# Scores of a causal chunk as three quarter blocks a head pair, and a chunk's values moved to the next iteration

## The chip, the core and the metric

The kernel runs on one core of a Trainium2 chip. The metric is the device time of one execution in microseconds (us); lower is better. Five engines run their own instruction streams in order: TensorE (PE, matmuls; PEld is its weight load), VectorE (DVE), ScalarE (ACT), GpSimdE (POOL) and SyncE (SP, which here only issues DMAs). They wait for each other by semaphores.

## The reference, cut to what matters

A linear attention with a complex, per-channel decay feeds a top-1 mixture of experts. Batch 4, 8 heads, 768 steps, 48 channels a head:

```python
for t in range(S):
    ar, ai = a_re_n[:, :, t, :, None], a_im_n[:, :, t, :, None]
    S_re, S_im = ar * S_re - ai * S_im + k_t (x) v_t, ar * S_im + ai * S_re
    y[:, :, t] = einsum('bhd,bhde->bhe', q[:, :, t], S_re)
...
e_idx = argmax(x @ w_gate, axis=1)          # x: y as 3072 rows of 384
for e in range(E):                          # 8 experts, 384 -> 1024 -> 384
    h = maximum(x[mask] @ w1[e], 0.0)
    out[mask] = gate_w * eom[mask, e] * (h @ w2[e])
```

## The kernel before, in words

The kernel has two stages. The attention stage (0 to about 272 us) walks over 24 chunks of 128 steps, six for each batch entry; the expert stage (about 283 us to the end) walks over eight experts. The change touches the first alone.

For chunk i, `main()` (L796) asks for these steps:

- `turn(i, "k")` and `turn(i, "q")` (L607): DVE multiplies the decayed k or q by cosine and sine (L611, tiles `kc`, `qc`), PE turns the eight heads (L95, into the PSUM banks `tr`, of which there are two), and ACT copies each bank of four heads out (L621, tiles `kt`, `qt`).
- `score(i, 0)` and `score(i, 1)` (L646), four heads each: PE makes a 128x128 matrix of keys by queries for each head (L653, PSUM tile `sc`), and DVE multiplies four of them by the causal mask (L654, 512 columns). Of each matrix the quarter with late keys and early queries is masked away.
- `state(i)` (L625): PE adds keys times values into the running state (L633, L638, tile `st`), in matmuls that give 32 partitions, and DVE scales it (L642).
- `values(i)` (L660): PE makes scores times values (L667) and queries times state (L673), heads in pairs. The even head's output lies on partitions 0 to 47 of the tile `xo`, the odd head's on 64 to 111. ACT copies it out (L677, `xt`).
- `finish(i)` (L682, L688) turns `xt` back (again into a `tr` bank) and stores it to `xd`; `gates(i)` (L233) and `chosen(i)` (a PE transpose of `ls`, L95, and L240) make the routing logits.

Beside this, groups of three chunks are prepared: logarithms, exponentials and arctangents on ACT and DVE, two running sums on PE (L510 and L563, tile `cs`), and a one-row `carry` from chunk to chunk, which is sent by a DMA that SP issues (L573) before DVE adds it into the next chunk (L545).

The order is not the order of the code. Within the attention loop a scheduler places the instructions of each engine, by a priority that follows from where `main()` and the side steps ask for them and by when it reckons that operands and buffers are ready. The stream it makes is fixed when the program is built; the engines then run it in order. After chunk 19 the lists of the first experts are made: table writes (L1059), the reading back of the lists, and the gather of expert 0's rows (L1104), which PE turns in L1012; the rows of the last two chunks come in through L763 (DVE) and L998 (PE). Then the experts begin (L1225).

## Time and profile before

| what | us |
|---|---|
| median of three runs (lowest, highest) | 530.51 (528.88, 531.61) |
| the profiled execution, its own time | 532.94 |
| its span in the trace | 531.1 |
| attention stage: last `xo` matmul begins | 272.0 |
| first expert matmul (L1225) | 283.12 |
| PE busy over the span | 493.5 |
| DVE busy, ACT busy | 337.3, 319.0 |

A "busy" time of PE contains the tail of each matmul, so that a busy PE isn't PE at its best pace; the time from one matmul's start to the next tells the pace. In the trace each fp32 matmul of the program, transposes aside, is two passes. A chain row gives a start, a length and what stood there, with the number of passes behind an x.

### The profile page before, as it was taken

To read this page: it belongs to the slowest core of one execution; us is meant where nothing else is said; L and a number is where in the kernel's file an instruction comes from. 1 tells how busy PE (TensorE), PEld (TensorE's weight loads), DVE (VectorE), ACT (ScalarE), POOL (GpSimd) and SP (SyncE) were. 2 spreads that over 40 slices of the span, in tenths; PEclk is the share of its full clock that TensorE was granted. 3 is DMA by queue.
4 is the path that set the end of the run, shared out by engine and by line. 5 is a ranking of instruction groups with operands and counts; after the bars stand their busy time and mean duration, and the time that the engine had idled before them with its cause. 6 is when DMAs were issued, how large, how long until landed. Compare 5 with 4: busy or idle time off the path is not lost.

```text
span 531.1 us, 11170 instructions
## 1 busy us (share of the span) xinstructions
PE 493.5 (93%) x4297; PEld 420.3 (79%) x4297; DVE 337.3 (64%) x775; ACT 319.0 (60%) x603; POOL 121.1 (23%) x131
## 2 busy tenths in 40 slices
PE   2799897998999999999899999999999999999992
PEld 0376565776777778878678889999999999999992
DVE  4578869895998899987685646355453726345220
ACT  7689678985879888767533447355453727354220
POOL 4000201030040503051350554412333222011112
PEclk9799989998999999999999999999999999999997
DMA  8664452534334321014560576525263644330001
GB/s 274 199 231 150 74 165 69 161 77 114 124 76 136 58 90 41 29 31 136 138 207 0 149 191 198 153 101 206 47 209 114 200 123 147 139 135 30 21 22 45
DMA packets 47523, 63.86 MB, mean 120 GB/s; under 512 B 12383, under 2 KB 39290, under 8 KB 47460
## 3 DMA queue, kind: packets, MB, share of 16 engines
q1 hardware_dynamic: 39332, 53.64, 33.8%
q0 software_dynamic: 8128, 9.42, 6.1%
q8 instruction: 36, 0.59, 0.5%
q14 instruction: 27, 0.22, 0.2%
HBM read 53.92 MB, written 9.88 MB: 120 GB/s over the span
## 4 chain that ended last, share of the span: by engine, by line
PE 57%; issue 17%; DMA 7%; DVE 7%; POOL 4%; ACT 4%; SPq 1%; POOLq 0%; DVEq 0%; ACTq 0%
PE up L1225 13%; PE acc L1163 12%; PE tr L95 8%; PE sc L653 4%; PE cs L563 4%; PE xo L667 3%; POOL out_dram L1176 3%; PE cs L510 3%; DMA carry<-ai 2%; PE xo L673 2%; PE st L638 2%; DMA ar<-in_a_re_dram 2%; PE cs L565 1%; POOL rows L1104 1%; PE xt L95 1%
## 5 line engine op out<-in xcount | busy, mean ns | idle before, releaser
L1230 DVE SCALAR_TENSOR_TENSOR hl<-up,hh 128x464 fp32r<-128x464 f32 (+7 forms) x64 | 37.7, 589 | 68.8 <-ACT hh L1229 67.5
L1229 ACT ACTIVATE hh<-up 128x464 fp32r<-128x464 f32 (+7 forms) x64 | 33.1, 518 | 74.0 <-PE up L1225 72.7
L1225 PE MATMUL up<-xh,w1h 128*128 128x464 f32 (+7 forms) x192 | 68.6, 357 | 0.0
L1225 PE MATMUL up<-xl,w1h 128*128 128x464 f32 (+7 forms) x192 | 67.6, 352 | 0.0
L1225 PE MATMUL up<-xh,w1l 128*128 128x464 f32 (+7 forms) x192 | 67.5, 351 | 0.0
L1163 PE MATMUL acc<-hh,w2h 128*128 128x464 f32 (+6 forms) x168 | 61.4, 366 | 0.0
L1176 POOL DMA_INDIRECT out_dram<-y,sid x28 | 31.8, 1135 | 124.5 <-ACT y L1198 121.6
L1163 PE MATMUL acc<-hl,w2h 128*128 128x464 f32 (+6 forms) x168 | 59.4, 356 | 0.0
L1163 PE MATMUL acc<-hh,w2l 128*128 128x464 f32 (+6 forms) x168 | 59.3, 353 | 0.0
L653 PE MATMUL sc<-qt,kt 96*128 96x128 f32 x384 | 51.2, 277 | 0.0
L653 PEld LDWEIGHTS sc<-qt,kt 96*128 96x128 f32 x384 | 47.3, 192 | 2.4 <-issue 1.1
L1104 POOL DMA_INDIRECT rows<-xd,sid x28 | 37.3, 1333 | 51.4 <-DVE w1l L203 22.6
L1059 POOL DMA_INDIRECT table<-entry,addr x20 | 31.4, 1571 | 65.3 <-DVE addr L1055 59.0
L203 DVE TENSOR_TENSOR w1l<-raw,w1h 128x512 fp32r<-128x512 f32 x48 | 30.5, 686 | 20.4 <-ACT w1h L202 17.3
L667 PE MATMUL xo<-scores,v 128*48 128x128 f32 x384 | 41.4, 279 | 0.0
L202 ACT CAST w1h<-raw 128x512 fp32r<-128x512 f32 x48 | 26.9, 619 | 17.0 <-DMA raw<-in_moe_w_dram 17.0
L1225 PEld LDWEIGHTS up<-xl,w1h 128*128 128x128 f32 x192 | 36.0, 188 | 1.2 <-DVE xl L1137 0.3
L1225 PEld LDWEIGHTS up<-xh,w1l 128*128 128x128 f32 x192 | 36.1, 188 | 1.0
L1225 PEld LDWEIGHTS up<-xh,w1h 128*128 128x128 f32 x192 | 36.1, 188 | 0.9
L203 DVE TENSOR_TENSOR w2l<-raw,w2h 128x512 fp32r<-128x512 f32 x48 | 30.5, 686 | 9.8 <-ACT w2h L202 7.4
L533 POOL COPY rcs<-rcs 24x48 f32<-24x48 f32 (+2 forms) x10 | 5.8, 579 | 134.0 <-DMA rcs<-re 86.9
L654 DVE TENSOR_TENSOR scores<-sc,mask 128x512 f32<-128x512 f32 x48 | 32.6, 681 | 5.0 <-PE sc L653 4.5
(214 smaller groups left out, 1125.2 us busy)
## 6 DMA issues: line engine op xcount, KB each, us to landing
raw<-in_moe_w_dram SPq DMA_DIRECT2D x32, 768.0 KB
ar<-in_a_re_dram SPq DMA_DIRECT2D x24, 192.0 KB
ai<-in_a_im_dram SPq DMA_DIRECT2D x24, 192.0 KB
k<-in_k_dram SPq DMA_DIRECT2D x24, 192.0 KB
q<-in_q_dram SPq DMA_DIRECT2D x24, 192.0 KB
v<-in_v_dram SPq DMA_DIRECT2D x24, 192.0 KB
xd<-xn SPq DMA_DIRECT2D x24, 192.0 KB
rows<-xd,sid POOLq DMA_INDIRECT x28
```

What stands on the lines that cost most here:

```text
L95: return nc.tensor.transpose(out=out, in_=in_, identity=ident[p0:p0 + n, p0:p0 + n])
L203: ins = nc.vector.tensor_tensor(out=lo[:, s], in0=raw[:, s], in1=hi[:, s].bitcast(F32), op=ALU.subtract)
L653: nc.tensor.matmul(sp[:, j * P:(j + 1) * P], r["kt"][:D2, h, :], r["qt"][:D2, h, :], start=True, stop=True)
L654: nc.vector.tensor_tensor(out=r["s"][:, 4 * hh:4 * hh + 4, :], in0=sp.rearrange("p (h t) -> p h t", t=P), in1=mask.unsqueeze(1).broadcast_ ...
L667: nc.tensor.matmul(op[u * DP:u * DP + D, j * P:(j + 1) * P], vt[c][:, h * D:(h + 1) * D], r["s"][:, h, :], start=True, stop=(cc == 0))
L1059: ins = nc.gpsimd.indirect_dma_start(out=table, out_offset=bass.IndirectOffsetOnAxis(ap=addr[:, c:c + 1], axis=0), in_=entry[:, c, :], in_ ...
L1104: nc.gpsimd.indirect_dma_start(out=rows[e % 2][:n, i, :], out_offset=None, in_=xd[:known], in_offset=bass.IndirectOffsetOnAxis(ap=ids[:n, ...
L1163: nc.tensor.matmul(accs[kt][:, :cap], w[:, cs], a, start=(ft == 0 and s == 0), stop=(ft == FT - 1 and s == 2))
L1176: ins = nc.gpsimd.indirect_dma_start(out=out, out_offset=bass.IndirectOffsetOnAxis(ap=ids(e)[:n, i:i + 1], axis=0), in_=y[:n, :], in_offse ...
L1225: nc.tensor.matmul(up[:, :cap], w[:, kt, :], x[:, kt, :], start=(m == 0), stop=(m == 3 * KT - 1))
L1229: nc.scalar.activation(out=hh, in_=up[:, :cap], func=AF.Relu)
L1230: nc.vector.scalar_tensor_tensor(out=hl, in0=up[:, :cap], scalar=0.0, in1=hh.bitcast(F32), op0=ALU.max, op1=ALU.subtract)
```

## The change

Three things are changed.

1. Scores. Keys and queries are cut in halves of 64. For each pair of heads (e even, o odd) four matmuls make 192 columns instead of 256: on partitions 0 to 63 the early keys of e with all queries and the late keys of o with the late queries, on partitions 64 to 127 the early keys of o with all queries and the late keys of e with the late queries. Each gives 64 partitions. The DVE mask works on 384 columns for four heads instead of 512, with a mask built of three blocks.
2. Values. For each pair the early queries take one matmul a head over all 128 partitions, with weights that are zero in the other head's half (`vz`), and the late queries one matmul a head, the even one with `v`, the odd one with a tile whose halves are swapped (`vs`). So a pair has four matmuls of 64 columns instead of two of 128. `vz` and `vs` are filled by four further DMAs a chunk; v arrives in memory with the even heads first. POOL builds the new mask and zeroes eight half tiles at the start.
3. Order of asking. `main()` asks in each iteration for values(i-1), score(i), state(i), gates(i-1), turn(i+1), finish(i-1) and chosen(i-1).

```diff
+            first_v = [pre.tile([P, H, D], F32, name=f"vz{n}") for n in range(VBUFS)]
+            for t in first_v:
+                nc.gpsimd.memset(t[HALF:, 0:HP, :], 0.0)
+                nc.gpsimd.memset(t[:HALF, HP:H, :], 0.0)
+            other_v = [pre.tile([P, HP, D], F32, name=f"vs{n}") for n in range(VBUFS)]
...
+            def loads_halves(i):
+                rows = v.rearrange("b (c x t) h d -> (b c) x t h d", x=2, t=HALF)[i]
+                z, o = first_v[i % VBUFS], other_v[i % VBUFS]
+                nc.sync.dma_start(out=z[:HALF, 0:HP, :], in_=rows[0, :, 0:HP, :])
+                nc.sync.dma_start(out=z[HALF:, HP:H, :], in_=rows[0, :, HP:H, :])
+                nc.sync.dma_start(out=o[:HALF], in_=rows[1, :, HP:H, :])
+                nc.sync.dma_start(out=o[HALF:], in_=rows[0, :, HP:H, :])
...
-                for j in range(4):
-                    h = 4 * hh + j
-                    nc.tensor.matmul(sp[:, j * P:(j + 1) * P], r["kt"][:D2, h, :], r["qt"][:D2, h, :], start=True, stop=True)
+                for j in range(2):
+                    e, o = 4 * hh + 2 * j, 4 * hh + 2 * j + 1
+                    kt, qt = r["kt"][:D2], r["qt"][:D2]
+                    to = sp[:, j * 3 * HALF:(j + 1) * 3 * HALF].rearrange("p (x t) -> p x t", t=HALF)
+                    parts = qt.rearrange("p h (x t) -> p h x t", t=HALF)
+                    nc.tensor.matmul(to[:HALF, 0:2, :], kt[:, e, :HALF], parts[:, e], start=True, stop=True)
+                    nc.tensor.matmul(to[HALF:, 0:3:2, :], kt[:, o, :HALF], parts[:, o], start=True, stop=True)
+                    nc.tensor.matmul(to[:HALF, 2, :], kt[:, o, HALF:], qt[:, o, HALF:], start=True, stop=True)
+                    nc.tensor.matmul(to[HALF:, 1, :], kt[:, e, HALF:], qt[:, e, HALF:], start=True, stop=True)
                 nc.vector.tensor_tensor(
-                    out=r["s"][:, 4 * hh:4 * hh + 4, :], in0=sp.rearrange("p (h t) -> p h t", t=P),
-                    in1=mask.unsqueeze(1).broadcast_to([P, 4, P]), op=ALU.mult)
+                    out=r["s"][:, 2 * hh:2 * hh + 2, :], in0=sp[:, :6 * HALF].rearrange("p (j t) -> p j t", j=2),
+                    in1=masks.rearrange("p x t -> p (x t)").unsqueeze(1).broadcast_to([P, 2, 3 * HALF]), op=ALU.mult)
...
                     for u in range(2):
-                        h = 2 * j + u
                         nc.tensor.matmul(
-                            op[u * DP:u * DP + D, j * P:(j + 1) * P], vt[c][:, h * D:(h + 1) * D], r["s"][:, h, :],
-                            start=True, stop=(cc == 0))
+                            op[u * DP:u * DP + D, j * P:j * P + HALF], vz[:, at_v(2 * j + u), :], by_block[:, 0, :],
+                            start=True, stop=(cc == 0), skip_group_check=True)
+                    for u in range(2):
+                        nc.tensor.matmul(
+                            op[u * DP:u * DP + D, j * P + HALF:(j + 1) * P], vs[:, j, :] if u else vt[c][:, j * D:(j + 1) * D],
+                            by_block[:, 1 + u, :], start=False, stop=(cc == 0), skip_group_check=True)
...
+                    if live(i - 1):
+                        yield from values(i - 1)
                     if live(i):
                         yield from score(i, 0)
                         yield from score(i, 1)
...
+                        yield from state(i)
+                    if live(i - 1):
+                        yield from gates(i - 1)
+                    if live(i + 1):
+                        need(i + 1)
+                        yield from turn(i + 1, "k")
+                        yield from turn(i + 1, "q")
+                    if live(i - 1):
+                        yield from finish(i - 1)
+                        yield from chosen(i - 1)
```

How the streams move is seen on PE, first, in the middle of the attention stage. Before, these eight rows follow each other there (`tr` are transposes, `sc` scores, `st` the state, `xo` the values; the numbers behind the names count buffers):

```order
L95 MATMUL tr_1883<-ident_71,kc1_162 96x128 x4
L653 MATMUL sc_1890<-qt0_165,kt0_166 128x128 x4
L95 MATMUL tr_1897<-ident_71,qc1_161 96x128 x4
L95 MATMUL tr_1907<-ident_71,qc1_161 96x128 x4
L653 MATMUL sc_1913<-qt0_165,kt0_166 128x128 x4
L95 MATMUL tr_1921<-ident_71,xt_1849 128x128 x4
L633 MATMUL st_1929<-state1_164,ident_71 96x384
L638 MATMUL st_1929<-v_937,kc0_160 32x48 x24
```

Four scores stand between the turns of k and of q, and all of these rows but the state's L638 give more than 64 partitions. The values follow further on as one block of pairs. Of the change, this is PE's stretch of the same kind, from the turn of k to the scores of the next chunk:

```order
L97 MATMUL tr_2163<-ident_71,kc1_168 96x128 x4
L538 MATMUL cs_2169<-l2_1794,tri_l_76 128x384
L97 MATMUL st_2199<-ident_71,ls_2153 128x128
L703 MATMUL xo_192<-scores_2094,vz2_173 48x64 x2
L707 MATMUL xo_192<-scores_2094,v_1013 48x64
L707 MATMUL xo_192<-scores_2094,vs2_185 48x64
L713 MATMUL xo_192<-qt0_187,state1_170 48x128
L97 MATMUL tr_2179<-ident_71,qc1_167 96x128 x4
L97 MATMUL tr_2185<-ident_71,qc1_167 96x128 x4
L713 MATMUL xo_192<-qt0_187,state1_170 48x128
L703 MATMUL xo_192<-scores_2094,vz2_173 48x64 x2
```

The scores no longer stand between the two turns; pieces of the values do, and the pair of L713 is parted by the turn of q. The end of the same stretch on PE, where the next scores begin:

```order
L713 MATMUL xo_192<-qt0_187,state1_170 48x128 x2
L703 MATMUL xo_192<-scores_2094,vz2_173 48x64 x2
L707 MATMUL xo_192<-scores_2094,v_1013 48x64
L707 MATMUL xo_192<-scores_2094,vs2_185 48x64
L591 MATMUL cs_2288<-ai_1195,tri_t_81 128x384
L713 MATMUL xo_192<-qt0_187,state1_170 48x128 x2
L684 MATMUL sc_2253<-qt1_189,kt1_190 64x128
L685 MATMUL sc_2253<-qt1_189,kt1_190 64x2x64
L686 MATMUL sc_2253<-qt1_189,kt1_190 64x64
```

Only the last part of the last pair stands in one run with the scores; a running sum (L591) stands ahead of it.

The second place is SP, around a carry. Before:

```order
L365 DMA v_1528<-in_v_dram 128x384
L573 DMA carry_1546<-ai_597 1x16x24
L365 DMA k_1858<-in_k_dram 128x384
L365 DMA q_1860<-in_q_dram 128x384
L365 DMA q_1988<-in_q_dram 128x384
```

With the change, a chunk's four half loads stand around it:

```order
L385 DMA v_1885<-in_v_dram 128x384
L410 DMA vz0_171<-in_v_dram 64x192
L601 DMA carry_1828<-ai_646 1x16x24
L411 DMA vz0_171<-in_v_dram 64x192
L412 DMA vs0_183<-in_v_dram 64x192
L413 DMA vs0_183<-in_v_dram 64x192
```

One of the half loads now stands between the load of v and the carry.

More of the change, by code (lines that the diff above doesn't have):

```diff
@@ L71, in tile_gated_attention_moe @@
     h3 = lambda t: t.rearrange("p (h d) -> p h d", d=D)
+    at_v = lambda h: h % 2 * HP + h // 2
+    HALF = P // 2
     const = ctx.enter_context(tc.tile_pool(name="const", bufs=1))
@@ L112, in tile_gated_attention_moe @@
     nc.gpsimd.tensor_copy(out=tri_o, in_=mask)
+    masks = const.tile([P, 3, HALF], F32, name="masks")
+    nc.gpsimd.memset(masks, 1.0)
+    for p0, blocks in ((0, (0, 2)), (HALF, (0, 1))):
+        for n in blocks:
+            nc.gpsimd.affine_select(
+                out=masks[p0:p0 + HALF, n, :], in_=masks[p0:p0 + HALF, n, :], pattern=[[1, HALF]], compare_op=ALU.is_ge,
+                fill=0.0, base=0, channel_multiplier=-1)
     tri_s = tri("tri_s", 1.0, strict=True, dt=BF16)
@@ L445, in prep_exp @@
                     if g == 0:
-                        spare = [wk.tile([P, H, P], F32, name="scores") for _ in range(2)] + [t[1] for t in turned_cats]
+                        spare = [wk.tile([P, HP, 3 * HALF], F32, name="scores") for _ in range(2)] + [t[1] for t in turned_cats]
                         st["spare"] = [t.rearrange("p h t -> p (h t)") for t in spare]
@@ L639, in state @@
                             sp[m:m + MS, h * D:(h + 1) * D], r["k"][:, h, :, :].rearrange("p a b -> p (a b)")[:, m:m + MS],
-                            d["v"][c][:, h * D:(h + 1) * D], start=(cc == 0), stop=True, skip_group_check=True)
+                            d["v"][c][:, at_v(h) * D:(at_v(h) + 1) * D], start=(cc == 0), stop=True, skip_group_check=True)
                 rcb = rc[:, i, :].unsqueeze(2).broadcast_to([D2, H, D])
@@ L674, in values @@
                                 op[u * DP:u * DP + D, j * P:(j + 1) * P], xs[:D2, h * D:(h + 1) * D], r["qt"][:D2, h, :],
-                                start=False, stop=True)
+                                start=False, stop=True, skip_group_check=True)
                 xt = wk.tile([P, HP, P], F32, name="xt")
@@ L796, in main @@
             def main():
-                late = []
                 for i in range(-1, NT + 1):
@@ L801, in main @@
                         fixed.enter_context(tc.manual_schedule(engines={mybir.EngineType.PE}))
-                    if live(i + 1):
-                        need(i + 1)
-                        for _ in turn(i + 1, "k"):
-                            yield
-                            while late:
-                                yield from chosen(late.pop())
+                    if live(i - 1):
+                        yield from values(i - 1)
                     if live(i):
                         yield from score(i, 0)
-                    if live(i + 1):
-                        yield from turn(i + 1, "q")
-                    if live(i):
                         yield from score(i, 1)
@@ L815, in main @@
                             yield from ratios(where[i][0])
-                    if live(i - 1) and i < NT:
-                        yield from finish(i - 1)
-                    n = 0
-                    for _ in chain(
-                            *([state(i)] if live(i) else []), *([gates(i - 1)] if live(i - 1) else []),
-                            *([values(i)] if live(i) else [])):
-                        n += 1
-                    if i == NT:
-                        yield from finish(i - 1)
-                    yield from (None for _ in range(n))
-                    if live(i - 1):
-                        late.append(i - 1)
-                    if i >= NT - 3:
-                        while late:
-                            yield from chosen(late.pop())
+                        yield from state(i)
[6 more added lines that the diff above has]
+                    if live(i - 1):
+                        yield from finish(i - 1)
+                        yield from chosen(i - 1)
                     if i == NT - 2:
@@ L884, in attention @@
                 todo += [(loads_a, g)] + [(loads_b, i) for i in range(starts[g], starts[g] + sizes[g])]
+            halves = list(range(2, NT))
             def loads():
+                while halves and st["done"] > halves[0] - VBUFS + 1:
+                    loads_halves(halves.pop(0))
                 while todo and st["early"] >= HOLD.get((todo[0][0] is loads_a, todo[0][1]), 0) and (st["phases"] > todo[0][1] - 3 if todo[0][0] is loads_a else st["done"] > todo[0][1] - AHEAD):
@@ L910, in attention @@
             loads_b(1, "v")
+            for i in range(2):
+                loads_halves(i)
             loads_b(2)
@@ L1303, in recurrence @@
                     for b in range(B):
-                        r = g * R + b * H
-                        nc.sync.dma_start(out=vt[r:r + H], in_=vv[b][:, bass.ds(t0, TB), :])
+                        for h in range(H):
+                            r = g * R + b * H + h
+                            nc.sync.dma_start(out=vt[r:r + 1], in_=vv[b][at_v(h):at_v(h) + 1, bass.ds(t0, TB), :])
                 ar, ai = tiles["ar"], tiles["ai"]
@@ L1446 @@
         a = _np.asarray(inputs[name])
-        a = _np.ascontiguousarray(a if name.startswith("moe") else a.transpose(0, 2, 1, 3))
+        if not name.startswith("moe"):
+            a = a.transpose(0, 2, 1, 3)
+        if name == "v":
+            a = _np.concatenate([a[:, :, 0::2], a[:, :, 1::2]], axis=2)
+        a = _np.ascontiguousarray(a)
         arrays[f"in_{name}_dram"] = a
```

5 lines of the change are left out of this document (4 added, 1 removed).

## The prediction

> **What bounds the kernel now.** I read the whole page first, then the busy time by stretches of 20 us, then the chain of waits inside the attention stage.
>
> ```profile
> span 531.1 us, 11170 instructions
> PE 57%; issue 17%; DMA 7%; DVE 7%; POOL 4%; ACT 4%; SPq 1%; POOLq 0%; DVEq 0%; ACTq 0%
> ```
>
> TensorE carries 57% of the chain, and the expert stage, from 283 us on, is nearly all of its own making. The change does not touch that stage, so the question is what the 283 us before it become.
>
> ```profile
> core 0: us, PE busy (x) PEld busy (x) DVE busy (x) ACT busy (x) POOL busy (x), PEclk, DMA share, GB/s
> 0.00:20.00 20.00, 7.02 (x10) 2.40 (x10) 9.20 (x22) 14.23 (x24) 6.39 (x39) 0.91 0.76 239
> 40.00:60.00 20.00, 19.42 (x267) 14.94 (x263) 18.43 (x47) 16.24 (x29) 3.40 (x3) 1.00 0.36 110
> 60.00:80.00 20.00, 17.08 (x88) 10.05 (x86) 13.31 (x31) 14.84 (x26) 0.00 (x0) 0.83 0.59 148
> 80.00:100.00 20.00, 16.40 (x182) 12.18 (x181) 17.68 (x38) 17.21 (x29) 1.82 (x2) 0.91 0.37 107
> 120.00:140.00 20.00, 17.88 (x219) 13.37 (x219) 13.72 (x34) 13.84 (x28) 0.00 (x0) 0.91 0.48 128
> 160.00:180.00 20.00, 20.00 (x257) 15.03 (x253) 17.30 (x49) 17.88 (x33) 2.16 (x2) 1.00 0.34 101
> 200.00:220.00 20.00, 20.00 (x245) 16.43 (x244) 18.42 (x40) 16.03 (x28) 4.55 (x4) 1.00 0.14 42
> ```
>
> The stage has two halves. Up to 100 us PE waits: for the first loads (DMA share 0.76), then for DVE and ACT, and its granted clock falls to 0.83. From 100 us on PE is busy 20.00 of 20 us, but for one hole at 120 to 140 us. There PE sets the pace, and DVE, at 17 to 18 of 20, follows close behind. So I cost the change in PE's own pace first.
>
> ```profile
> 100.28 1.79 PE sc L653 x16
> 104.70 0.64 PE st L638 x34
> 116.78 0.35 PE xo L667 x4
> 117.14 0.22 PE xo L673 x4
> 117.36 0.22 PE xo L667 x4
> ```
>
> These rows of the chain give the pace. Sixteen passes of scores, 128 columns each, take 1.79 us: **0.112 us** a pass. Values come in pairs, on 64 partitions each, and four passes take 0.22 us: 0.055 a pass, so two run side by side. The state's passes of 48 columns go three abreast. And the first four passes of values after matmuls of another width take 0.35 in place of 0.22: a **change of width costs 0.13 us** (widths: up to 32, up to 64, and more partitions of output; the sums with 32 rows of input count apart).
>
> **Scores.** Before: 24 chunks x 16 passes x 0.112 = 43.0 us. After: for each pair of heads two steps of 128 columns and two of 64, each step both halves side by side. For 64 columns no row stands here; the nearest is the state's with 48: (0.64 - 0.13) / (34 / 3) = 0.045 a step. Between that and 0.112 at 128 columns, by the columns, lies 0.057, which I take; the ends are 0.045 and 0.112. So 24 x 4 x 2 x (0.112 + 0.057) = 32.4: **-10.6 us** (ends -12.9 and 0).
>
> **Values.** A pair had two steps of 128 columns and gets four of 64: 24 x 4 x (4 x 0.057 - 2 x 0.112) = **+0.4** (ends -4.2 and +21.5).
>
> **Changes of width.** The order counts them. Up to the last `xo` matmul there are 163 before and 234 with the change: the values are asked for early, but they are placed in pieces between the turns of k and q, where the scores stood before, and each piece is 64 wide among transposes 128 or 96 wide. 71 x 0.13 = **+9.2** (ends 0, if every change falls where PE would have waited, and 9.2). Pieces cut a pair as well, so that one half runs without the other: runs with unequal halves rise from 22 to 58, the time lost by that from 2.5 to 4.4 us at the paces above: **+1.9**.
>
> Sum for PE: -10.6 + 0.4 + 9.2 + 1.9 = +0.9 us. The saving is eaten by the changes of width. It also lies unevenly. For chunks 8 to 23, where PE sets the pace, the same count gives -7.1 + 0.3 + 55 x 0.13 + 1.7 = **+2.0 us**; what chunks 0 to 7 gain, 1.1 us, falls where PE waits anyway and counts for nothing.
>
> The Trainium skill (TensorEngine Tiling (Array Packing), Key Properties) says that changing the tiling mode, not just the tile, drains the engine; the trace agrees, with the 0.13 us above. By a reading without that rule PE's sum would be -8.3 us.
>
> The Trainium skill (TensorE: Matmul & The Clock Gate, Part 3, The mechanism) also says that a weight load overlaps matmuls in flight only when the row group differs. The two halves here share all rows; by that rule the score halves would go one behind the other, and the sum would be that of rival E. The next rows speak against it.
>
> ```profile
> L667 PE MATMUL xo<-scores,v 128*48 128x128 f32 x384 | 41.4, 279 | 0.0
> L667 PEld LDWEIGHTS xo<-scores,v 128*48 128x48 f32 x384 | 26.0, 122 | 7.0 <-issue 5.3 <-ACT re L223 0.5 <-DVE ai L456 0.2
> L654 DVE TENSOR_TENSOR scores<-sc,mask 128x512 f32<-128x512 f32 x48 | 32.6, 681 | 5.0 <-PE sc L653 4.5 <-issue 0.2
> L568 DVE TENSOR_TENSOR ai<-cs,rnd 128x384 f32<-128x384 f32 x24 | 13.2, 549 | 0.3
> L621 ACT COPY kt<-tr 96x512 f32<-96x512 f32 x48 | 26.3, 584 | 5.1 <-PE tr L95 5.0
> ```
>
> A value's weight load lasts 0.122 us and its pass starts every 0.055: the load is hidden, halves with shared rows included.
>
> **DVE.** The 48 masks go from 512 to 384 columns: 0.681 to the 0.549 of L568, which also reads 384 columns from PSUM. 48 x 0.132 = 6.3 us less DVE time. It counts where DVE and what follows it set the pace, in 40 to 100 us, not under a full PE: 16 masks of chunks 0 to 7 x 0.132 = **-2.1** (ends 0 and -6.3).
>
> **The hole at 120 us.**
>
> ```profile
> 120.31 4.38 DMA carry<-ai
> 124.71 0.56 DVE ai L545
> 125.31 1.18 PE cs L563 x2
> DVE ai L545 <- DMA carry<-ai: 5.7, 5, 3.1
> PE cs L563 <- DVE ai L545: 3.5, 4, 2.1
> POOL rcs L519 <- ACT re L223: 8.0, 2, 6.9
> L545 DVE SCALAR_TENSOR_TENSOR ai<-carry,ai 1x384 f32<-1x384 f32 x15 | 8.1, 541 | 5.7 <-DMA carry<-ai 5.7
> 163.34 1.28 SPq L365 DMA_DIRECT2D ai<-in_a_im_dram  x3
> ```
>
> PE stands for the carry there, and the clock is low after it: in 120 to 140 us PE loses 2.1 us of busy time, and about as much again to a clock of 0.91. Whether the new order meets the same hole I cannot tell from the order; I take **-1.5** (ends 0 and -4.2). SP gets 96 more DMAs, each 1.28 / 3 = 0.43 us of issue, and a half load can stand ahead of a carry; DVE waited for five of its fifteen carries. At the start 12 half loads (3 chunks x 0.19 MB = 0.6 MB, 2.5 us at 239 GB/s) go in among loads that PE needs only later; POOL's new memsets fit into the 6.9 us for which it waits. Together **+0.6** (ends 0 and +6.5: fifteen carries x 0.43).
>
> **The end of the stage.**
>
> ```profile
> 248.01 0.24 DVE logits L240
> 272.85 5.41 DMA rows<-xd,sid
> 278.31 1.37 PE sc L1012 x10
> 280.57 1.71 PE sc L998 x8
> 277.45 0.95 DVE L763 TENSOR_SCALAR row<-iota,rank,ohp 128x464 fp32r<-128x464 f32 x2
> ```
>
> Two ways end together: the lists, which start from the logits of chunk 19, wait for the gather until 278.31 and take L1012 then; the rows of the last two chunks are ready at 278.40 (L763). In the new order the transpose of chunk 19's logits stands ahead of chunk 20's values and turns. If the gather comes a microsecond or two sooner, L1012 runs without its wait, and L998 begins about 279.5 in place of 280.57: **-1.0** (ends 0 and -2.2, the distance from 278.40).
>
> **Sum:** +2.0 - 2.1 - 1.5 + 0.6 - 1.0 = -2.0 us. The profiled execution took 532.94 (span 531.1 and 1.8 around it), so 530.9; the median of the runs is 2.43 lower, 530.51, and gives **528.5**.
>
> **The rivals.**
>
> A. The forecast: PE's gain goes into changes of width. Speaks for it: PE at 20.00 of 20 and the count of 234. 526 to 531, chance 0.42.
>
> B. PE loses its waits as well: all of DVE's 6.3 us counts, the hole at 120 us is gone (4.2), the end gains 1.2, against +2.0: -9.7, so 520.8. For it: values now fill what the turns wait for, and masks get a whole turn of time. Against: PE has little waiting left after 130 us. Chance 0.22.
>
> C. Slower: the two `tr` banks. A turn of q can begin only when ACT has copied k's first bank out, 0.584 us after its turns end; before, four scores (0.9 us) stood between, now one or two pieces of values (0.3 to 0.5 us with their changes). That suffices with ACT free. If ACT is busy with another piece of work, PE stands; it decides from the point where the copy starts over 0.3 us late in most chunks. At 0.5 us a chunk: 16 x 0.5 = +8, so 536.5. Against: such waits are small before.
>
> ```profile
> PEld tr L95 <- ACT kt L621: 3.3, 7, 1.3
> ```
>
> Seven waits, 3.3 us, are the start of it. Chance 0.25.
>
> D. The half loads hold up the carries: each of fifteen by one issue of 0.43, +6.5, so 535. Chance 0.07.
>
> E. The change does not do what it says: the score halves run one after the other. Then the scores take 24 x 4 x 4 x (0.112 + 0.057) = 64.9 us, 32.5 over the sum above: 561. The values' pairs speak against it. Chance 0.04.
>
> **How the numbers follow.** Under 0.5% (2.65 us, about what a measurement of this kernel tells from no change) lies 527.86 to 533.16. A puts 0.19 below and 0.22 within (0.01 above); B 0.20 below and 0.02 within; C 0.08 within and 0.17 above; D 0.02 within and 0.05 above; E 0.04 above. Sums: faster 0.39, same 0.34, slower 0.27. A's own range is 526 to 531; with B down to 520 and C up to 539 about 0.18 is left out.
>
> **What would show it.** Chain rows of 16 or 32 score passes at 0.028 to 0.085 us a pass bear out the halves; the first passes of each piece of values after a transpose, 0.13 late, bear out the widths; DVE's mask group at 0.55; PE still 20.00 of 20 in most stretches after 130 us (A) or with waits for `kt` and `qt` of 0.2 to 0.6 us in most chunks (C). The forecast is wrong if changes of width cost nothing inside a wait (B), or if PE's busy time after 130 us falls below 19 of 20 (C, D).

## The result and the profile after

| | before | after |
|---|---|---|
| median of four runs each, us (lowest, highest) | 531.06 (528.88, 532.77) | **545.09** (544.44, 546.10) |
| ratio, 95% interval | | **1.0268** (1.0225 to 1.0311) |
| the profiled execution, its own time; its span | 532.94; 531.1 | 544.44; 542.5 |
| mean granted clock of the profiled execution | 0.975 | 0.966 |

The changed kernel is slower by 14 us. 528.5 was forecast, with a range of 526 to 531; with rivals B and C it went from 520 to 539. A ratio is estimated from the executions of a kernel that agree with each other, so here and below it is not the quotient of the medians beside it. Where the time comes from is seen best by setting the start of ACT's copies of `xo` (`xt`, L677 before, L717 after: one a chunk) against each other. All times are us of the profiled execution:

| stretch | before | after |
|---|---|---|
| start to the copy of chunk 0 | 33.1 | 34.3 |
| copy of chunk 0 to that of chunk 8 | 99.0 | 98.5 |
| chunk 8 to chunk 20 | 115.1 | 117.0 |
| chunk 20 to chunk 23 | 25.2 | **33.3** |
| chunk 23 to the end | 258.6 | 259.4 |

So of the 11.4 us between the spans, 8.1 lie in three chunks. The busy time by stretches of the changed kernel shows the same place from the other side:

```profile
core 0: us, PE busy (x) PEld busy (x) DVE busy (x) ACT busy (x) POOL busy (x), PEclk, DMA share, GB/s
60.00:80.00 20.00, 17.37 (x151) 9.57 (x150) 12.76 (x27) 12.07 (x18) 0.00 (x0) 0.74 0.65 181
80.00:100.00 20.00, 15.55 (x180) 11.46 (x180) 18.21 (x41) 16.40 (x31) 7.52 (x3) 0.91 0.37 92
160.00:180.00 20.00, 19.41 (x320) 14.78 (x320) 17.29 (x49) 17.98 (x34) 0.80 (x2) 1.00 0.44 131
200.00:220.00 20.00, 19.72 (x302) 15.18 (x301) 17.94 (x43) 16.90 (x32) 4.49 (x4) 1.00 0.24 64
250.00:260.00 10.00, 6.41 (x111) 5.03 (x110) 4.52 (x22) 3.07 (x8) 2.92 (x3) 0.81 0.55 179
260.00:270.00 10.00, 10.00 (x185) 8.15 (x184) 5.57 (x10) 6.99 (x15) 0.00 (x0) 0.85 0.43 124
270.00:280.00 10.00, 7.54 (x93) 5.94 (x93) 6.86 (x21) 5.41 (x12) 5.23 (x4) 0.84 0.59 176
280.00:290.00 10.00, 9.33 (x72) 7.68 (x72) 4.14 (x20) 2.06 (x5) 0.32 (x1) 0.65 0.59 159
```

The stretches from 160 and from 200 us read much as before: PE at 19.4 and 19.7 of 20, before 20.00. From 250 us on PE stands for a third of a stretch and then runs at a lower granted clock, down to 0.65. Before, the same four stretches had a clock of 1.00 throughout; the first and the last of them:

```profile
250.00:260.00 10.00, 9.28 (x132) 7.54 (x131) 9.09 (x26) 4.75 (x11) 4.49 (x3) 1.00 0.47 124
280.00:290.00 10.00, 10.00 (x52) 8.97 (x51) 6.29 (x16) 3.90 (x8) 0.00 (x0) 1.00 0.00 0
```

The chain of the changed kernel shows the two stands (start, length, what stood there):

```profile
250.97 0.47 ACT xn L739
251.43 5.84 another core or an unknown queue x2
257.29 0.27 ACT ls L247
257.61 1.09 PE tr L97 x4
...
269.68 3.32 DMA slots<-table
273.00 0.51 issue
273.51 1.66 ACT w2h L214 x3
275.17 0.49 ACT qt L649
275.70 0.32 PE sc L684
```

PE's turns of k at 257.61 had waited 3.8 us for a `tr` bank, which the logits in it kept until ACT copied them out (`ls`, L247) at 257.29. ACT stood for 5.8 us for something that the trace can't name. The second stand, 2.2 us, ends at 275.70: the copy of q's turn (L649) stood on ACT behind three casts of expert weights (L214), and those behind a transfer (the chain names the reading back of the lists).

What the first stand waits for is seen on DVE, in the view of one line, the scaling of chunk 21's state (L670):

```profile
L670 DVE TENSOR_TENSOR state<-st,rc x1: 555/555/555, 255.8 to 255.8; 96x384 f32<-96x384 f32 x1
  remote: 2.6, 1
```

The last recorded pass of this state on PE ends at 253.23; DVE starts at 255.81. In the trace no signal of PE stands between 252.44 and 255.79, and the next two stand at 257.21 and 257.27, although the passes for the logits end in the records at 253.45. So PE's results were signalled 2.6 to 3.8 us after the ends in their records, and DVE, ACT and at last PE itself waited for them.

### The profile page after: what moved, and what is told of

It reads as the page before. It is cut to its first block, busy times and chain, and to the rows that moved or that the text cites. A ratio compares the mean times of both kernels' runs of the same rounds, so it can differ in the third digit from the quotient of the medians.

```text
span 542.5 us, 12857 instructions
## 1 busy us (share of the span) xinstructions
PE 499.3 (92%) x5065; PEld 417.3 (77%) x5065; DVE 331.0 (61%) x775; ACT 318.1 (59%) x603; POOL 124.9 (23%) x144
## 4 chain that ended last, share of the span: by engine, by line
PE 56%; issue 16%; DVE 9%; DMA 7%; ACT 5%; POOL 3%; another core or an unknown queue 1%; SPq 0%; POOLq 0%; DVEq 0%; ACTq 0%
PE acc L1196 10%; PE up L1258 10%; PE tr L97 9%; DMA carry<-ai 4%; PE cs L591 4%; PE xo L713 3%; POOL out_dram L1209 3%; PE cs L538 2%; PE xo L703 2%; PE st L666 2%; PE sc L684 2%; DMA raw<-in_moe_w_dram 2%; PE xo L707 1%; PE st L661 1%; PE cs L593 1%
## 5 line engine op out<-in xcount | busy, mean ns | idle before, releaser
L1262 ACT ACTIVATE hh<-up 128x464 fp32r<-128x464 f32 (+7 forms) x64 | 33.1, 517 | 73.0 <-PE up L1258 68.7
L1092 POOL DMA_INDIRECT table<-entry,addr x20 | 34.2, 1708 | 105.8 <-DVE addr L1088 102.2
L1137 POOL DMA_INDIRECT rows<-xd,sid x28 | 35.2, 1258 | 64.9 <-DVE w1l L215 27.6
L713 PE MATMUL xo<-qt,state 96*48 96x128 f32 x320 | 43.4, 288 | 0.0
L215 DVE TENSOR_TENSOR w2l<-raw,w2h 128x512 fp32r<-128x512 f32 x48 | 30.5, 687 | 14.0 <-ACT w2h L214 11.4
L703 PE MATMUL xo<-scores,vz 128*48 128x64 f32 x384 | 38.1, 233 | 0.1
L1258 PEld LDWEIGHTS up<-xh,w1l 128*128 128x128 f32 x192 | 36.1, 188 | 1.0
L1258 PEld LDWEIGHTS up<-xh,w1h 128*128 128x128 f32 x192 | 36.1, 188 | 0.9
L97 PE MATMUL tr<-ident,kc 128*96 128x128 f32 x192 | 31.5, 300 | 5.5 <-ACT ls L247 4.6
L684 PE MATMUL sc<-qt,kt 96*64 96x128 f32 x192 | 34.3, 277 | 2.2 <-ACT qt L649 2.0
L214 ACT CAST w2h<-raw 128x512 fp32r<-128x512 f32 x48 | 26.8, 622 | 14.7 <-DMA raw<-in_moe_w_dram 11.1
L591 PE MATMUL cs<-ai,tri_t 128*128 128x384 f32 x48 | 25.0, 612 | 11.0 <-ACT trig L235 4.4
```

Source lines behind the costliest of these rows:

```text
L97: return nc.tensor.transpose(out=out, in_=in_, identity=ident[p0:p0 + n, p0:p0 + n])
L215: ins = nc.vector.tensor_tensor(out=lo[:, s], in0=raw[:, s], in1=hi[:, s].bitcast(F32), op=ALU.subtract)
L591: nc.tensor.matmul(tp[:, :HD], tri_t, fr, start=True, stop=first or not plain)
L684: nc.tensor.matmul(to[:HALF, 0:2, :], kt[:, e, :HALF], parts[:, e], start=True, stop=True)
L703: nc.tensor.matmul(op[u * DP:u * DP + D, j * P:j * P + HALF], vz[:, at_v(2 * j + u), :], by_block[:, 0, :], start=True, stop=(cc == 0), sk ...
L713: nc.tensor.matmul(op[u * DP:u * DP + D, j * P:(j + 1) * P], xs[:D2, h * D:(h + 1) * D], r["qt"][:D2, h, :], start=False, stop=True, skip_ ...
```

## The experiments

The theories at the start: the loss is the stand near 254 us and what follows from it (first rival: it is the new order as such, or the halves as such). Later, as stretches of half clock showed in the profiles with the stand, the clock became a theory of its own.

The letters in the expectations name the theories of the time; F is throughout the late piece of PE's program, of which more below.

### The changed kernel again, on four chips

The edit is none: the same program, profiled and timed beside the kernel before, each time on another chip (which one the result came from isn't noted). In `e5_after_again`:

> The changed kernel once more, as the control of the next two. Both theories: 543.5 to 546.5, TensorE's hole between 250 and 260 us again, and the granted clock at 0.5 behind it.

In `e9_after_third`:

> The changed kernel a third time, on the chip of the next three. It took 544.4 to 546.1 on the first chip (4 runs) and 533.2 to 544.0 on another (10 runs), where the late piece of program came late as well and no hole followed: theory F is dead. Theory T (the last chunks): up to chunk 20 the change is worth nothing either way; in the new order the weights are asked for about 6 us later against chunk 19 than before (8.4 us after its xt copy, before 2.3), so their splits and the reading of the lists fall among the last chunks' copies on ScalarE and TensorE stands; whether the sum of the stands tips the clock gate differs from run to run. Expected here: 533 to 546, in the profile a stand of over 1.5 us between 250 and 285 us with half clock behind it whenever the time is above 536.

In `e13_after_fourth`:

> The changed kernel, on the chip of the next three. If this chip is like the first and the one of the third run: 543 to 548, VectorE's state of chunk 21 over 2 us after the end of its passes, TensorE's hole of 3.8 us behind it. If it is like the other: 533 to 544, that distance 0.4 us.

In `e17_after_fifth`:

> The changed kernel once more, to be set beside the next run on the same chip. It has shown two sizes: on two chips 533 to 540 (PE's state results of chunk 21 come about 0.4 us after the last recorded matmul, no hole), on two 543 to 548 (2.6 us after it, a hole of 3.8 us near 254 to 258 and half clock behind it). Theory H (the hole is a second loss, on top of a steady one): 536 to 539 without the hole, 543 to 546 with it, and nothing between. Rival N (the two sizes are scatter of one loss): the state results come about 0.4 us late and the time is over 541, or 2.6 us late and the time is under 540.

| run | this, us | before, us | ratio (95%) | chunks 8 to 20 | 20 to 23 | state's results late | half clock, us |
|---|---|---|---|---|---|---|---|
| before, profile above | | 531.06 | | 115.1 | 25.2 | | 13.7 |
| after, the result | 545.09 | 531.06 | 1.0268 (1.0225 to 1.0311) | 117.0 | 33.3 | 2.58 | 30.7 |
| e9_after_third | 543.83 | 531.14 | 1.0268 (1.0197 to 1.0338) | 117.3 | 32.1 | 2.67 | 30.7 |
| e5_after_again | 538.42 | 532.26 | 1.0092 (1.0043 to 1.0141) | 115.2 | 24.8 | 0.42 | 23.9 |
| e13_after_fourth | 536.53 | 532.30 | 1.0103 (1.0034 to 1.0173) | 115.9 | 25.2 | 0.42 | 17.1 |
| e17_after_fifth | 536.34 | 532.19 | 1.0063 (1.0021 to 1.0104) | 117.1 | 24.3 | 0.43 | 23.9 |

("Late" is DVE's start of L670 in chunk 21 less the end of PE's last recorded pass; "half clock" is how long the trace's record of the granted clock stood at 0.5 between 40 and 500 us of the profiled execution.)

`e5` was expected at 543.5 to 546.5 with the stand, and had neither. So there are two losses, as far as one profiled execution of each set and its median tell. **One comes alone in three of the five sets**: 4 to 6 us, ratios 1.006 to 1.010. **The other came in two of the five**, the result and `e9`: PE's results 2.6 us late, a stand of 3.8 us, a second one of 1.9 to 2.2 us, and 7 to 8 us more in three chunks. Without it the same DVE line reads, in `e13_after_fourth`,

```profile
L670 DVE TENSOR_TENSOR state<-st,rc x2: 541/548/554, 251.3 to 259.6; 96x384 f32<-96x384 f32 x2
  PE tr L245: 0.5, 1
```

and its stretches have neither stand nor half clock:

```profile
250.00:260.00 10.00, 9.90 (x221) 7.80 (x219) 7.88 (x17) 6.84 (x14) 3.85 (x3) 1.00 0.65 201
280.00:290.00 10.00, 10.00 (x55) 9.07 (x55) 5.41 (x14) 3.88 (x8) 0.00 (x0) 1.00 0.05 20
```

In `e5` and `e17` there is no stand at 254 us either, but half the clock is gone from 280 us on. The last stretch of `e17_after_fifth`:

```profile
280.00:290.00 10.00, 9.60 (x39) 8.72 (x40) 1.85 (x3) 2.12 (x4) 0.00 (x0) 0.66 0.06 21
```

The chains say why. Ahead of these rows stands the gather of expert 0, until 278.26 before. In `e13_after_fourth`:

```profile
270.75 8.38 DMA rows<-xd,sid
279.14 0.04 issue
279.18 1.37 PE sc L1045 x10
```

and in `e17_after_fifth`:

```profile
270.82 9.53 DMA rows<-xd,sid
280.35 0.04 issue
280.40 3.13 PE sc L1045 x12
```

The chain counts the gather from its last issue (in `e17` from the last but one), and so the 8.38 and 9.53 can't be set against the 5.41 of before. From its first issue to its end the gather takes 12.8 us before, and 13.8, 13.5 and 13.0 in `e5`, `e13` and `e17`; in all four the same two weight loads are issued 0.8 and 2.6 us behind that first issue. What came no sooner is its start: 265.42 before, and 266.11, 265.62 and 267.32, although the logits of chunk 19 stood at 244.52 to 246.39 in place of 248.01. From logits to gather 20.9 to 21.1 us pass, before 17.4. Of the 3.6 us or so, 1.5 lie ahead of the reading back of the lists (logits to its first issue 15.3 us in place of 13.8), and 2.0 to 2.2 in it: from SP's first issue to DVE's first operation on the lists it takes 4.4 to 4.6 us in place of 2.4. SP's queue shows what lies beside it, first before and then in `e13`:

```profile
257.23 0.37 SPq L188 DMA_DIRECT2D raw<-in_moe_w_dram  x1
261.84 3.88 SPq L1078 DMA_DIRECT2D slots<-table  x8
```

```profile
259.23 0.37 SPq L200 DMA_DIRECT2D raw<-in_moe_w_dram  x1
259.85 5.97 SPq L1111 DMA_DIRECT2D slots<-table  x8
```

The last weight load ahead of the reading was issued 4.6 us ahead of it before, and 0.6 us ahead in the changed kernel; the DMA share is 0.17 from 262 to 264.25 us before, and 0.93 to 0.95 from 259 to 263 us in `e13`. The profiles of all runs agree: in the five in which that load was issued 4.6 us or more ahead (before, `e3`, `e10`, `e12`, `e16`) the reading takes 1.5 to 2.4 us, in `e4` with 2.6 us ahead 3.1, and in the other fourteen with 0.6 to 0.8 us ahead 4.0 to 6.5. No run moved that load alone.

PE stands 2.0 us in `e17` and `e5`, and the clock halves for 6.8 us within 0.4 us of the stand's end; in `e13` it stands 1.1 us, and the clock holds.

The clock as a theory can be put to all runs. The result and these four runs have 29 comparable executions of the changed kernel, and the four runs 58 of the kernel before; their means are 539.1 and 532.0 us. Span times granted clock, a bookkeeping figure for the work at full clock, is 521.6 after against 519.9 before in the mean: **+1.7 us**. The mean clock is 0.971 against 0.980, and 1% of 532 us is 5.3. So three quarters of the 7.1 us go with a lower granted clock, on which the prediction had no term. Within the 29, time and clock go together (correlation -0.88); this is accounting, and does not show by itself which of the two leads.

### One part alone

**`e3_halves_only`**: scores and values by halves, asked for in the order of before.

```diff
-                    if live(i - 1):
-                        yield from values(i - 1)
...
+                            *([state(i)] if live(i) else []), *([gates(i - 1)] if live(i - 1) else []),
+                            *([values(i)] if live(i) else [])):
```

> The changed kernel with the order of asking of before: scores and values by halves, but turns of k, scores, turns of q, scores, and a chunk's values in its own round. Changes of width in the attention stage, counted alike for all: 140 before, 220 changed, 248 here. The prediction's arithmetic: scores -10.6, values +0.4, changes (248 - 140) x 0.13 = +14.0: TensorE +3.8, so chunk 20's rows (its xt copy) come 2 to 5 us later than the 239.9 of before, and the time is 533 to 537 if no hole opens in the last chunks. Rival (changes cost little when they fall into a wait): xt of chunk 20 by 237 or sooner, time 524 to 529.

543.75 us, ratio 1.0187 (1.0098 to 1.0276): above the 533 to 537 that were expected, and dearer than the whole change where the latter has no stand. From chunk 8 to 20 it needs 121.6 us against 115.1: its matmuls change width for 17.0 us there (before 9.5), and PE stands 7.6 (before 5.2).

**`e4_order_only`**: whole scores and values as before, in the new order (an edit of the kernel before).

```diff
+                    if live(i - 1):
+                        yield from values(i - 1)
                     if live(i):
                         yield from score(i, 0)
...
-                            *([state(i)] if live(i) else []), *([gates(i - 1)] if live(i - 1) else []),
-                            *([values(i)] if live(i) else [])):
```

> The kernel before with only the new order of asking: whole scores and values, a chunk's values one round later with the next scores. Changes of width 208 against 140, and nothing saved: 68 x 0.13 = +8.8 for TensorE at most, so chunk 20's xt 4 to 9 us after 239.9 and the time 535 to 540. Rival (the new order itself hides waits): chunk 20's xt within 1 us of 239.9, time 529 to 532; then the halves bring the 0.9 to 2.5 us that the chunks up to 20 lost.

537.86, ratio 1.0106 (1.0041 to 1.0171): the time as expected, while the copy that stood at 239.9 came at 242.9, 3.0 us later and not 4 to 9. The new order alone brings most of the changes of width, 14.4 us of them from chunk 8 to 20 against 9.5, and takes waits away (2.6 against 5.2). The stand near 254 us isn't there. Neither part gains by itself, and each brings changes of width; together they bring 15.0 us, less than the halves alone.

**`e8_values_whole`**: in the changed kernel, a greater urgency for values keeps a chunk's pieces together.

```diff
-            UG = {}
+            UG = {"values": 300}
```

> The changed kernel with a chunk's values asked for ahead of all else once their scores are masked: they run whole among scores and state and not in pieces between the turns. Changes of width 166 in place of 220, no half left alone. The prediction's price: 54 x 0.13 + 1.9 = 8.9 us less for TensorE, so, without a hole in the last chunks, 528 to 532 (from the 537 of the shifted kernels). Rival (the pieces filled waits, and whole values leave TensorE standing at the turns): TensorE's idle time in the stage grows by as much as the changes shrink, 535 to 540.

542.73, ratio 1.0165 (1.0082 to 1.0249), a miss. The changes of width fell as meant, from 28.2 to 21.5 us over the chunks 0 to 23, but PE's waits rose by more: from chunk 8 to 20 11.0 us, against 3.4 to 4.9 in the five profiles of the changed kernel. The pieces of values are what fills the time until ACT has copied a turn; the price of a change is the price of that filling. This alone does not make 542.73, though: chunk 8 to 20 takes 118.4 us, 1.1 to 3.2 more than in the five, and chunk 20 to 23 takes 36.1, 11 more than where the changed kernel has no stand. There ACT's copies stand behind casts of expert weights, and those behind a weight load; PE stands 2.4 us until 273.88, and half clock of 6.8 us begins at 275.35. So the end of the stage decides this run too.

### Where the instructions stand

The late results came with a piece of PE's program: every 256 of its instructions one 16 KB packet of the program is fetched, and the one due near chunk 21 came late, behind a weight load. Theory: PE stands for its program. Tiny matmuls at PE's start move all that follows against these pieces.

```diff
-            warm(ident, W0)
+            warm(ident[:, :8], 32)
```

> The changed kernel with 32 tiny matmuls (8 columns, into a bank that is not read) ahead of the attention stage. Each is two passes with a weight load each, so TensorE's program is 128 instructions longer at its front; behind row 40 every engine's order is that of the changed kernel, row for row. Theory F (late program): the loss of the last chunks begins where TensorE ran out of program. Its program arrives in pieces of 16 KB, one for every 256 instructions; the piece of 253.1 to 254.3 us stands behind a load of 768 KB of weights and comes after 439 instructions in place of 256. With the shift it falls due about 3 us earlier, before that load starts (0 packets in 246 to 250 us), so TensorE's hole at 253.9 to 257.6 goes, the granted clock is 1.00 from 250 to 290 us, and the time is 534 to 537. Rival G (the new order: banks, ScalarE's queue, the split of the weights): the order is the same, so the hole stays where it is, with the clock of 0.8 behind it, and the time is 543.5 to 546.5.

> The same with 16 tiny matmuls, 64 instructions. Theory F: the piece falls due about 1.5 us earlier, just ahead of the load; no hole between 250 and 260 us, time 534 to 537, unless another piece now meets a load. Rival G: 543.5 to 546.5, as without the shift.

The first two were marred: each tiny matmul waited for the one before (0.65 us), and the copy of chunk 0 began at 51.6 and 42.1 us in place of 34.3, so that the times, 553.69 and 545.02 (ratios 1.0424, 1.0346 to 1.0501, and 1.0233, 1.0161 to 1.0305), say nothing of the end; from chunk 0 to 23 both lie at 239.3 to 239.5, against 248.8 in the result, without the stand. For the next ones the matmuls are independent:

```diff
-            warm(ident, W0)
+            wp = pp.tile([P, 512], F32, name="st", bufs=1); [nc.tensor.matmul(wp[:, :8], ident, ident[:, :8], start=True, stop=True) for _ in range(16)]
```

> The shift by 64 instructions without the price that it had at the front: 16 tiny matmuls into one bank, all ahead of TensorE's first real matmul, where it waits for its inputs; behind them every engine's order is that of the changed kernel. Theory F: no hole and no half clock between 250 and 260 us; xt of chunk 23 at 273 to 276 us in place of 283.1, time 535 to 539. Rival G: 543.5 to 546.5. Rival H (the two shifts so far gained in the last chunks only because the front was late): the front is not late here, so 543.5 to 546.5 too.

> The same with 64 tiny matmuls: 256 instructions, one whole piece, so every later instruction stands at the same place in its piece as in the changed kernel. Theory F: the hole of the last chunks comes back where it was, with the half clock behind it; set against the first xt copy, chunk 23's comes 247 to 250 us later (changed kernel: 283.1 - 34.3 = 248.8; the shifts by 64 and 128: 239.5 and 239.3). Rival H: it stays at 239 to 241. The front may be late by the tiny matmuls, 0 to 8 us.

`e6` gave 536.79, ratio 1.0041 (1.0001 to 1.0081). `e7`, with 64 of them, which put the pieces back in their old place, lost 18 us at the start (555.79, ratio 1.0413, 1.0321 to 1.0505), but from chunk 0 to 23 it took 243.7 and had no stand in chunk 21, where the theory of the program piece wanted 247 to 250 (and its rival 239 to 241). And in `e5_after_again`, `e13_after_fourth` and `e17_after_fifth`, with no shift at all, the same piece landed as late (194 to 197 instructions past the point where it was due, as in the result) without a stand. **That theory fell.** Twice more:

> The shift by 64 instructions ahead of the first real matmul, once more, on the chip of the changed kernel. Theory F in its weaker form (where the program's pieces fall decides, but only on some chips): distance 0.4 to 0.5 us, no hole, 534 to 538 on any chip. Rival (the chip alone decides): as the changed kernel on this chip, within 2 us, hole included.

> The changed kernel with sixteen more tiny matmuls on PE at the start, which move every later instruction of PE's stream by 64 against the blocks in which the stream is fetched. Twice before it gave 534.6 and 536.8, but on chips on which the changed kernel itself shows no hole, or was not run. If this chip shows the hole for the changed kernel: theory P (the place of the instructions in the stream decides) expects 533 to 538 and no hole here; rival Q (the chip decides) expects the hole here too and 541 to 546. If this chip shows no hole: both expect 533 to 538, and the question stays open.

534.61, ratio 1.0062 (1.0027 to 1.0097), and 536.52, ratio 1.0070 (1.0030 to 1.0109). None of the three chips on which this shift of 64 (`e6`, `e14`, `e18`) was timed shows the stand for the changed kernel itself, so whether a shift takes it away was not tried on a chip that has it.

### Attempts at a mend

Five edits of the changed kernel aim at the end of the stage or at PE's state passes. `e10_old_tail` has the old order from round 17 on (`SWAP = 17`); `e12_old_tail_early_whole` has this and whole values in chunks 0 to 7; `e11_pace` lets the side steps run ahead faster; `e15_state_whole` makes the state in matmuls of 96 partitions in place of three of 32; `e16_pace_state_whole` has both of the last.

```diff
-            PACE = 0.52
+            PACE = 0.64
...
-            MS = 32
+            MS = 96
```

> The changed kernel whose rounds 17 to 24 ask in the order of before (chunk 16's values first, then turns of k, scores, turns of q, scores, the chunk's own values); rounds before that in the new order, halves everywhere. Theory T: the weights' first load is asked for 2 to 5 us after chunk 19's xt copy, TensorE's first up matmul starts 43 to 44.5 us after that copy (before 43.1, changed kernel 45.3 to 53.3), time 531 to 535. Rival W (the width changes of the halves cost the end): 230 changes against 220, so the end is no better than the changed kernel's on this chip.

> The changed kernel with the side work (gates, lists, the weights' first loads) asked for faster: 0.64 of its steps for each step of the main line in place of 0.52; order of the main line and halves as in the changed kernel. Theory T: the weights come earlier against chunk 19, the end is shorter, first up matmul 43 to 45 us after chunk 19's copy, time 532 to 537. Rival W: as the changed kernel on this chip, within 2 us.

> As e10, and the values of chunks 0 to 7 ahead of all else as in e8, whose first xt copy came at 30.7 us against 34.1, and chunk 8's 97.3 us behind it against 98.6: 4.7 us less than e10, so 527 to 531, faster than the kernel before if e10 is at 532 or below. Rival (whole values leave TensorE standing there too): as e10.

> The changed kernel whose state is summed in 8 matmuls of 96 columns of k for a chunk and not in 24 of 32: 16 passes in place of 48, a third of the instructions, same result. Theory S (the hole begins in the burst of 128 + 96 instructions of scores and state within 2.3 us, which TensorE is not supplied with in time): distance at chunk 21 below 1 us, no hole, and changes of width 206 in place of 220 (-1.8): 533 to 537. Rival (chip or loads): as the changed kernel on this chip, less 1.8.

> The same with the faster side work of e11 (534.3 against 543.8 for the changed kernel on one chip). Theory T and S together: weights asked for earlier, casts of the second piece between the copies of chunks 20 and 22, changes of width 204: 530 to 534, level with the kernel before or faster. Rival (side work only moves the stands): 536 or more.

| run | this, us | ratio (95%) | chunks 0 to 8 | 8 to 20 | 20 to 23 |
|---|---|---|---|---|---|
| e10_old_tail | 540.52 | 1.0150 (1.0073 to 1.0227) | 99.9 | 120.9 | 25.1 |
| e11_pace | 534.26 | 1.0041 (0.9998 to 1.0084) | 98.4 | 115.3 | 27.5 |
| e12_old_tail_early_whole | 541.25 | 1.0205 (1.0147 to 1.0262) | 103.9 | 117.4 | 25.3 |
| e15_state_whole | 545.98 | 1.0265 (1.0180 to 1.0349) | 102.1 | 122.4 | 24.6 |
| e16_pace_state_whole | 539.86 | 1.0165 (1.0088 to 1.0242) | 105.0 | 115.9 | 23.3 |

Only `e11` came within what was expected; the others lie 5 to 11 us above. On the chip of the first three, `e9` had needed 98.8, 117.3 and 32.1 us for these stretches. The old order in the last rounds takes the stand at the end away, and gives half of that back ahead of it (120.9 in place of 117.3); whole values in the first chunks cost 5 us there. The state in whole matmuls made the state's line itself slower, the opposite of what was expected:

```profile
L666 PE MATMUL st<-v,kc 128*96 128x48 f32 x320 | 31.7, 253 | 0.0
L666 PEld LDWEIGHTS st<-v,kc 128*96 128x96 f32 x320 | 31.3, 171 | 4.7 <-issue 4.3 <-DMA k<-in_k_dram 0.2
```

A weight load lasts 0.171 us here (`e15`), in place of 0.111 for 32 partitions, and the passes no longer go three abreast: one starts every 0.085 us, before three every 0.043. `e11_pace` is the best version: on the chip on which the changed kernel took 543.83, it took 534.26, though the late result is there too (its L670 waited 3.5 us, PE stood 2.0 at 254.06). Its mean clock was 0.983, that of before beside it 0.982. No version was faster than the kernel before.

## Why the prediction was wrong, point by point

The step that failed is the end of the stage, put at -1.0 us: from the copy of chunk 20 to the end of the span the result took 8.9 us more than before (33.3 and 259.4 against 25.2 and 258.6). The work of PE, on which the forecast was built, came out nearly as counted.

**PE's pace: right.** The chain of the changed kernel, as the values of chunk 8 end and the scores of the next begin, shows the paces:

```profile
131.88 0.19 PE xo L707
132.06 0.23 PE xo L713 x4
...
132.79 0.11 PE sc L685
...
132.90 0.06 PE sc L685
132.95 0.06 PE sc L686
133.01 0.05 PE sc L687
133.06 0.06 PE sc L684
133.12 0.11 PE sc L685
```

The row of L713 has four passes in 0.23 us, two side by side, as before. In the scores a head pair has eight passes, from the L685 at 132.79 to that at 133.12, 0.33 us: two steps of 0.11 and two of 0.055, which is both halves side by side. 0.057 was taken for a step of 64 columns. **Rival E** (one half after the other) was wrong. From chunk 8 to 20, PE's work outside waits and changes fell by 3.0 to 3.6 us (forecast for 12 of its 16 chunks: -7.1 + 0.3 + 1.7, of which three quarters are -3.8), and the changes of width rose from 9.5 to 15.0, by 5.5 (forecast 55 x 0.13 x 3/4 = 5.4). Their price can be seen in PE's starts: in these chunks the first start behind a change comes 0.09 us later than the pass ahead of it accounts for (mean of 75 changes before and of 116 in the result), and in the values at 116.71 the first pair takes 0.04 us more than the next, 0.140 in place of 0.103. The waits went from 5.2 to 3.4 to 4.9. The sum, waits included, is +0.1 to +2.2 us over the five profiles and holds the 1.5 that follow from the forecast's +2.0 for 16. That the saving is eaten by the changes of width, the core of **rival A**, the forecast, stood; the time it gave didn't, by what follows. One reading was too strong: before, PE isn't at 20.00 of 20 in every stretch from 100 us on but for the hole; five of the stretches that the prediction doesn't print, up to 260 us, hold 18.89 to 19.67.

**DVE: the operation right, the gain wrong.**

```profile
L688 DVE TENSOR_TENSOR scores<-sc,masks 128x384 f32<-128x384 f32 x48 | 25.9, 550 | 4.6 <-PE sc L687 4.4
DVE ai L573 <- DMA carry<-ai: 7.2, 5, 2.7
PEld tr L97 <- ACT kt L649: 2.7, 8, 0.6
```

The mask takes 0.550, as said (0.549). But -2.1 was counted for chunks 0 to 7, and from chunk 0 to 8 the five profiles gained 0.2 to 1.3 us. In those chunks the granted clock fell as well: 0.74 from 60 to 80 us, against 0.83 before, with 10.2 us at half clock in place of 6.8.

**The hole at 120 us: wrong.** -1.5 was taken, and SP's issues +0.6. The wait for the carry is still there at 124.83 (5.51 us on the chain, before 4.38). DVE's waits for carries come to 7.2 us in the result and to 4.4 to 8.5 us over the five profiles, four to eight times, before 5.7 and five times. That is on both sides of before, so of **rival D**'s +6.5 no sign is shown.

**The end of the stage: wrong, sign included.** -1.0 was taken, since the logits were thought to come sooner and the gather with them. The logits did, by 1.6 to 3.5 us in the three sets without the late results; the gather didn't, since the reading of the lists had come to lie beside a weight load. The rows of L1045 begin at 279.18 to 280.40 there, those of L1012 before at 278.31: +0.9 to +2.1. From there to the first expert matmul it is 4.8 us before and in `e13`, but 7.9 and 8.4 in `e5` and `e17`, where the clock halves for 6.8 us: 3.0 to 3.6 more. The step counted where a transpose stands; it did not look at when SP issues the weight loads that come to lie beside the reading of the lists. The prediction counted 96 more DMAs on SP, and none that moved. In the result and in `e9` the late results come on top, 7 to 8 us in chunks 20 to 23, and their cause stays open.

**Rival B** was wrong for these reasons: the waits of chunks 8 to 20 shrank by 0.3 to 1.8 us only, and the hole and the end gained nothing. **Rival C**, the nearest in size, 536.5, is not what happened: the waits of PE's turns for `kt` are 2.7 us (2.7 to 3.1 over the five profiles), before 3.3. The times of 536 to 538 in three sets came from elsewhere.

**What was missing.** The prediction had read that PE's clock falls to 0.83 where PE waits, and the term of the hole counted 2.1 us of stand and about as much for the clock. For the end of the stage no term and no rival had the granted clock. A stand of 2 us at the end of the stage costs its 2 us and half of 3.4 to 10.2 us behind it. In two sets there is the second loss besides, a stand out of results that PE signals late, and for that no row of before gave notice.

**Open** is why PE's results of chunk 21 come 2.6 us late in two sets of five, and in `e11_pace` beside one of them. The late program piece doesn't do it alone (`e5`, `e7`). Traffic of weight loads isn't needed either: in `e11_pace` DVE waited for the state from 250.1 to 253.6 us while the DMA share from 250 to 254 was 0.04. Shown is only what follows from it. In both sets, three table writes of POOL (L1092), 0.97 us each, lie across the stand (253.0 to 256.5 in the result); in the three others the first of them starts as far ahead of the state's end, 0.2 us, and nothing stands. No run took them away.

## What to carry to other kernels

A tuned order that replaces long runs of one matmul shape by short pieces of several pays for every seam: count the seams before the columns. Before the end of a stage is priced, look up when each queue issues the large loads of the next stage, since a load that stood well ahead of a small transfer may come to stand just ahead of it, and the small one may be what the stage waits for. Price a stand of TensorE with the clock behind it, and time a change of a per cent on more than one chip.

## What was not expected of the hardware

**The clock after a stand.** From 240 to 297 us of all profiles, PE sat idle for 1.80 us and more (up to 3.73) eight times, and each time half clock, of 3.4, 6.8 or 10.2 us, began in the stand or within 2 us of its end. Of three stands of 1.71 to 1.74 us two went with it and one, in `e3` until 271.83, did not; five of 1.30 to 1.45 did not, and one stretch of half clock, in `e7`, began 6.4 us behind a stand of 1.43. So length alone doesn't decide near 1.7 us. The Trainium skill (TensorE: Matmul & The Clock Gate, Part 1, What's actually happening) has the clock decided in windows of 3413 ns that run freely; the lengths here agree, being multiples of 3.4 us. The summary of the Trainium skill's page (TensorE: Matmul & The Clock Gate, Why this matters for your kernels) warns of gaps over about 3 us; here 1.7 to 1.9 us were enough.

**One program, two sizes.** One program took 536.3 to 538.4 us on three chips and 543.8 on a fourth, while the kernel before lay at 531.1 to 532.3 on all four. Chip and moment can't be told apart here, since each chip was used once.
